# Products of a zeroed tile in f32 with 128 columns in place of bf16 with 512

## The chip, the cores and the metric

The kernel runs on one core of a Trainium2 chip. The core has a matrix engine (TensorE, PE in the profile, with its weight loads as PEld), a vector engine (VectorE, DVE), an activation engine (ScalarE, ACT), a general engine (GpSimd, POOL) and an engine that here only issues transfers (SyncE, SP). Each runs its own list of instructions in order; they wait for each other by semaphores. The metric is the device time of one execution in microseconds. Before the change it is 210.38 us, the median of 3 runs (210.37 to 210.68).

## The reference

Attention over 4 sequences of 768 tokens with 8 heads of 64, followed by two matrix products with a softplus between them:

```python
q, k, v: (4, 8, 768, 64); n_global, n_local = 8, 96
scores = q @ k.T / 8 - slope[h] * dist        # dist = |i - j|, or 96 for a global key outside the window
keep   = (j < 8) | ((i - j >= 0) & (i - j < 96))
a      = softmax(where(keep, scores, -1e9))
x      = (a @ v) as (3072, 512)
h      = x @ w_in                             # w_in: (512, 2048)
g      = max(h, 0) + log1p(exp(-|h|))
out    = g @ w_out                            # w_out: (2048, 512)
```

Inputs and outputs are float32.

## The kernel before, in words

The 3072 tokens are cut into 24 blocks of 128. Two neighbouring blocks form a unit (12 of them), whose q, k and v are loaded as f32, cast to bf16, and q and k are brought into the layout in which the head's dimension lies on the partitions: for the first three units by transposes on TensorE (L792 and L810, products with a permuted identity), for the later ones by transposing transfers. Each block then goes through scores (L897 and L950 `scores`, with a bias that is either added by DVE, L976, or put into PSUM first by a product with the identity, L887 and L931), exp on ACT (L910, L983), the product with v (L1002), the division by the row's sum (DVE, L1013 and L1014) and a transpose back (L1033, evicted at L1038).

Two blocks form a group of 256 tokens (12 groups). `mm1` (L1060) multiplies a group by w_in, eight steps of two 128-column pieces, and ACT makes the softplus of it (exp at L1075, log at L1086). The second product is L1107 for the first two groups, and L522, with sums of blocks made at L452, for the others. w_in and w_out arrive as 16 loads of 512 KB, issued on SP (L640) into a ring of f32 buffers and cast into place (L644).

The order of every engine's work is written out by hand in the string `ORDER`: a name and a letter for the engine each. Semaphores are put in from the reads and writes that each step states. Among the names are `blank`, a memset of a tile by DVE (L1159), and `fill0` to `fill34` (L1234), 35 products of that zeroed tile with itself on TensorE. They stand only in the first 21 us: `fill0` to `fill12` ahead of everything else on TensorE, the other 22 singly, in twos and in threes between the transposes, scores and products with v of the first blocks, the last three (`fill32` to `fill34`) ahead of `a0.2`, the third step of the first group's `mm1`. Each writes the PSUM tile `x_ps`, which nothing reads until a later product has begun it anew. Names that the steps below use: `sb0.0` is the bias product at L887, `trq` and `trk` are transposes, `sc` scores, `pv` the product with v, `xt` the transpose back, `cin` a cast of a w_in piece.

Of the kernel before, what the change touches and what calls it, by code (L numbers as in the profile page):

```python
# [12 lines left out]
F32 = mybir.dt.float32  # L13
BF16 = mybir.dt.bfloat16
# [6 lines left out]
class Program:  # L21
# [6 lines left out]
    def op(self, name, eng, dur, rank, fn, reads=(), writes=(), after=(), dma=None, sync=(), count=1,  # L28
           port=False, alts=None, mutex=None):
        o = Op()  # L30
        o.name, o.eng, o.fn, o.sync, o.ins = name, eng, fn, list(sync), None
        if alts:
            o.eng = self.placed[name]
            assert o.eng in alts, (name, o.eng)
            o.fn = lambda: fn(o.eng)
        assert o.eng == self.placed[name], name
        deps = set(after) | set(sync)
        for t in reads:
            if t in self.writer:
                deps.add(self.writer[t])  # L40
        for t in writes:
            if t in self.writer:
                deps.add(self.writer[t])
            deps.update(self.readers.get(t, ()))
        for t in reads:
            self.readers.setdefault(t, []).append(o)
        for t in writes:
            self.writer[t] = o
            self.readers[t] = []
        deps.discard(o)  # L50
        o.deps = deps
        assert name not in self.ops, name
        self.ops[name] = o
        return o
# [194 lines left out]
def kernel(  # L249
# [11 lines left out]
    nc = tc.nc  # L261
    P = nc.NUM_PARTITIONS
# [29 lines left out]
    const = ctx.enter_context(tc.tile_pool(name="const", bufs=1))  # L292
# [6 lines left out]
    x_ps = ps.tile([P, 512], F32, name="x_ps")  # L299
# [28 lines left out]
    ident = const.tile([P, P], BF16, name="ident")  # L328
    ident_p = const.tile([P, P], BF16, name="ident_p")
    ident_q = const.tile([P, P], BF16, name="ident_q")  # L330
    blank = const.tile([P, 512], BF16, name="blank")
    rel, far, dist = (
        raw_t[NRAW - 1][:, 256 * x : 256 * x + 256].rearrange("p (a t) -> p a t", a=2) for x in range(3)
    )
# [56 lines left out]
    def users(key):  # L391
        return ([pl.writer[key]] if key in pl.writer else []) + list(pl.readers.get(key, ()))
# [838 lines left out]

    def fillers(js):
        def fn():
            nc.tensor.matmul(x_ps[:], blank[:, 0:P], blank[:])  # L1234

        for j in js:
            last = op(f"fill{j}", "PE", 0.216, 1e6 + j, fn, reads=["blank"], after=users(("x",)))
            pl.writer[("x",)], pl.readers[("x",)] = last, []
# [150 lines left out]
```

## Time and profile before

| | |
|---|---|
| median of 3 runs | 210.38 us (210.37 to 210.68) |
| the profiled execution's own time | 210.5 us |
| its span, first to last instruction | 208.6 us |
| PE busy | 201.1 us, 96% |
| ACT, DVE, POOL busy | 172.9, 159.9, 103.9 us |
| the 32 recorded products of the zeroed tile | 11.0 us on PE, 1.2 to 20.6 us |
| weight loads | 2211 |

Lengths are in us where nothing else is said. Products overlap in the pipeline: the length of one (mean 454 ns for the zeroed tile) is longer than the distance from one start to the next, and the distance is what a row of them costs. A bracket behind a row of the timeline says how long the engine sat idle ahead of it and what ended that. The chain of waits is followed back from the last instruction to what released each step.

### The profile page before, as it was taken

How to read it: one execution, taken by the hardware profiler on the slowest of the kernel's cores; microseconds unless marked ns; L12 is line 12 of the kernel's file. 1: busy time of each engine (PE TensorE's matmuls, PEld its weight loads, DVE VectorE, ACT ScalarE, POOL GpSimd, SP SyncE). 2: the span in 40 equal slices, each digit the busy share in tenths (PEclk: the TensorE clock that was granted, in tenths of full speed). 3: DMA queues.
4: the chain of work that ended last, by engine and by line, in shares of the span. 5: the costliest groups of instructions: out<-in, count | busy, mean ns of one | idle time of the engine just before them, and what ended most of it. 6: DMA issues, size and time to landing. Idle time of an engine off the chain costs nothing.

```text
span 208.6 us, 5495 instructions
## 1 busy us (share of the span) xinstructions
PE 201.1 (96%) x2202; PEld 164.7 (79%) x2211; DVE 159.9 (77%) x302; ACT 172.9 (83%) x254; POOL 103.9 (50%) x107
## 2 busy tenths in 40 slices
PE   7999899999998999999999999999999999999993
PEld 2465787666767889888988888888888889888882
DVE  5878889999869896786997897927897784434373
ACT  4788999899998999999799999679879895897300
POOL 4064683327886532546062179865707506623540
PEclk9999999999999999999999999999999999999999
DMA  5999999999999998999899969965641304200205
GB/s 172 365 361 388 387 357 363 336 240 237 205 178 231 240 199 204 244 310 200 198 176 287 245 149 227 249 135 126 103 76 28 126 5 134 71 0 0 104 16 187
DMA packets 70649, 40.99 MB, mean 196 GB/s; under 512 B 30432, under 2 KB 62688, under 8 KB 70624
## 3 DMA queue, kind: packets, MB, share of 16 engines
q1 hardware_dynamic: 69936, 39.99, 79.5%
q10 hardware_dynamic: 688, 0.66, 1.0%
q8 instruction: 17, 0.28, 0.6%
q14 instruction: 8, 0.07, 0.1%
HBM read 27.26 MB, written 6.29 MB: 161 GB/s over the span
## 4 chain that ended last, share of the span: by engine, by line
PE 74%; DMA 11%; DVE 8%; SPq 2%; issue 1%; POOL 1%; ACT 1%; ACTq 0%; POOLq 0%; DVEq 0%
PE h_ps L1060 34%; PE o_ps L522 23%; DMA raw<-in_moe_w_in_dram 5%; PE x_ps L1002 4%; PE s_ps L950 4%; PE s_ps L1107 3%; DMA kT<-kb 3%; DMA raw<-in_v_dram 2%; PE o_ps L1107 2%; PE x_ps L522 2%; DVE z L976 2%; DMA out_dram<-osb 1%; PE s_ps L522 1%; DVE vb L707 1%; SPq L640 1%
## 5 line engine op out<-in xcount | busy, mean ns | idle before, releaser
L1060 PE MATMUL h_ps<-XT,w_in_bf 128*128 128x256 bf16 x768 | 94.0, 273 | 1.3 <-DMA XT<-xs 0.6
L1060 PEld LDWEIGHTS <-w_in_bf 128*128 128x128 bf16 x768 | 73.4, 98 | 12.8 <-DMA XT<-xs 0.7
L1075 ACT ACTIVATE e<-h_ps 128x512 f32<-128x512 f32 x96 | 59.4, 635 | 13.7 <-PE h_ps L1060 13.0
L1086 ACT ACTIVATE g<-e 128x1024 bf16<-128x1024 f32 x48 | 49.6, 1051 | 0.5
L976 DVE TENSOR_TENSOR z<-s_ps,biasA 128x1024 f32<-128x1024 f32 x38 | 45.8, 1217 | 2.6 <-PE s_ps L950 1.9
L983 ACT ACTIVATE pb<-z 128x1024 bf16<-128x1024 f32 (+1 forms) x44 | 43.2, 992 | 1.9 <-DVE z L976 1.4
L452 POOL TENSOR_TENSOR g<-g 128x1024 bf16<-128x1024 bf16 x11 | 24.1, 2194 | 31.1 <-DVE raw L452 30.9
L522 PEld LDWEIGHTS <-g 128*128 128x128 bf16 x320 | 30.8, 98 | 3.6
L452 POOL TENSOR_TENSOR raw<-g 128x1024 bf16<-128x1024 bf16 x8 | 17.5, 2182 | 19.3 <-ACT g L1086 13.3
L522 PEld LDWEIGHTS <-raw 128*128 128x128 bf16 x240 | 22.7, 98 | 2.7
L522 PE MATMUL o_ps<-raw,raw 128*128 128x256 bf16 x192 | 24.4, 273 | 0.0
L452 DVE TENSOR_TENSOR raw<-g 128x1024 bf16<-128x1024 bf16 x22 | 16.8, 770 | 5.6 <-ACT g L1086 3.5
L1002 PEld LDWEIGHTS <-pb 128*128 128x128 bf16 x352 | 16.4, 98 | 4.2 <-ACT pb L983 0.5
L522 PE MATMUL o_ps<-raw,g 128*128 128x256 bf16 x160 | 19.6, 273 | 0.0
L1014 DVE TENSOR_TENSOR xs<-x_ps,rcp 128x256 bf16<-128x256 f32 x40 | 17.0, 424 | 1.4
L1002 PE MATMUL x_ps<-vb,pb 128*128 128x65 bf16 x304 | 15.8, 193 | 0.2 <-DVE xs L1014 0.2
L522 PE MATMUL o_ps<-w_out_bf,g 128*128 128x256 bf16 x128 | 15.8, 273 | 0.0
L675 POOL CAST qb<-raw 128x1024 bf16<-128x1024 f32 x8 | 9.7, 1215 | 10.4 <-DMA raw<-in_q_dram 8.7
L707 POOL CAST vb<-raw 64x512 bf16<-64x512 f32 x20 | 13.6, 680 | 2.3 <-DMA raw<-in_v_dram 1.5
L868 POOL COPY vb<-vb 4x512 bf16<-4x512 bf16 x18 | 11.7, 649 | 5.0 <-PE x_ps L1002 4.3
L1013 DVE RECIPROCAL rcp<-x_ps 128x4 f32<-128x4 f32 x40 | 7.1, 178 | 7.6 <-PE x_ps L1002 7.1
L1234 PE MATMUL x_ps<-blank 128*128 128x512 bf16 x32 | 11.0, 454 | 1.5 <-DVE blank L1159 1.2
(125 smaller groups left out, 225.6 us busy)
## 6 DMA issues: line engine op xcount, KB each, us to landing
raw<-in_v_dram SPq DMA_DIRECT2D x12, 512.0 KB, 5.5
out_dram<-osb SPq DMA_DIRECT2D x22, 256.0 KB, 3.4
raw<-in_q_dram SPq DMA_DIRECT2D x9, 512.0 KB, 5.1
raw<-in_k_dram SPq DMA_DIRECT2D x9, 512.0 KB, 5.9
raw<-in_moe_w_in_dram SPq DMA_DIRECT2D x8, 512.0 KB, 9.1
raw<-in_moe_w_out_dram SPq DMA_DIRECT2D x8, 512.0 KB, 9.2
raw<-in_k_dram SPq DMA_DIRECT2D x6, 256.0 KB, 5.9
raw<-in_q_dram SPq DMA_DIRECT2D x4, 256.0 KB, 7.1
```

What stands on the lines that cost most here:

```text
L452: (nc.vector if eng == "DVE" else nc.gpsimd).tensor_tensor(dst, a[0], b[0], ALU.subtract)
L522: nc.tensor.matmul(psum(j), lhs[:, f // 2, f % 2, :], w(f), start=(f == 0 and not (chain and j in "267")), stop=(f == 7), skip_group_check ...
L707: copy_on[eng](dst, src)
L868: copy_on[eng](vb_of(prev)[sl, :, 0:D], vb_of(first)[sl, :, 0:D])
L976: nc.vector.tensor_tensor(z, src, bias, ALU.add)
L983: nc.scalar.activation(pb[:, 0:nr, :].rearrange("p (y a) b -> p y (a b)", y=2), src, AF.Exp, scale=1.0 / root_d)
L1002: nc.tensor.matmul(xv[:, h, :], pb[:, 4 * (h % 2) + 2 * part + h // 2 if lone else u_all * (2 * (h % 2) + h // 2) + u, :], vb_of(prev if u ...
L1014: nc.vector.tensor_tensor(xs[:, 4 * part : 4 * part + 4, :], xv[:, :, 0:D], rcp[:][:, :, None].to_broadcast([P, 4, D]), ALU.mult,)
L1060: last = nc.tensor.matmul(hv[:, j, :], w_in_bf[:, m, fb * P : fb * P + P], XT[g % NXG][:, m, :], start=(m == 0), stop=(m == NM - 1),)
L1075: nc.scalar.activation(e[:, p % 2, :, :].rearrange("p j (b t r) -> p (j b) r t", b=2, r=2), hb[:].rearrange("p (a r t) -> p a r t", a=4, r=2),
L1086: nc.scalar.activation(gt[:, 2 * p - 2 : 2 * p + 2, :].rearrange("p a t -> p (a t)"), e[:].rearrange("p a j t -> p (a j t)"), AF.Ln, bias=1.0,
L1234: nc.tensor.matmul(x_ps[:], blank[:, 0:P], blank[:])
```

## The change

The zeroed tile becomes 128 x 128 in f32 (512 bytes in a partition) where it was 128 x 512 in bf16 (1024 bytes). Each product takes the whole tile as both operands and writes 128 columns of `x_ps`, where it took 128 columns as weights and all 512 as the moving operand.

```diff
-    blank = const.tile([P, 512], BF16, name="blank")
+    blank = const.tile([P, P], F32, name="blank")
 ...
     def fillers(js):
         def fn():
-            nc.tensor.matmul(x_ps[:], blank[:, 0:P], blank[:])
+            nc.tensor.matmul(x_ps[:, 0:P], blank[:], blank[:])
 
         for j in js:
             last = op(f"fill{j}", "PE", 0.216, 1e6 + j, fn, reads=["blank"], after=users(("x",)))
```

`ORDER` and all other steps stay as they are. In the program's list for TensorE a product of bf16 is two rows, a weight load and the product; a product of f32 is one row, with no load written for it. The first place is the head of TensorE's list (before with -, after with +; the counts and waits stand at the row):

```order
-L1234 LDWEIGHTS blank [waits DVE_49]
-L1234 MATMUL x_ps<-blank 128x512
+L1234 MATMUL x_ps<-blank 128x128 [waits DVE_49]
+L1234 MATMUL x_ps<-blank 128x128 x12
 L887 LDWEIGHTS ident [waits DVE_49,Pool_49]
 L887 MATMUL h_ps_64<-bias_127,ident 128x256 [waits Activation_49]
```

The wait for the memset moves from the load to the product; 13 pairs, of which the first is shown, become 13 rows, still ahead of the bias product of `sb0.0`.

The second place is `fill13`, between `sb0.0` and the first transposes of q, which wait for DVE's cast:

```order
 L887 MATMUL h_ps_65<-bias_127,ident 128x256 [waits Activation_49]
-L1234 LDWEIGHTS blank
-L1234 MATMUL x_ps<-blank 128x512
+L1234 MATMUL x_ps<-blank 128x128
 L792 LDWEIGHTS qb_81 [waits DVE_49]
 L792 MATMUL s_ps_61<-ident_q,qb_81 128x2x32x2 [waits Activation_49]
```

No row around it moves and no wait is added; the same holds at every other place. On DVE one row changes, the memset (counted in 32-bit words there):

```order
 L1384 UNCONDITIONAL_BRANCH
-L1159 MEMSET blank 128x256
+L1159 MEMSET blank 128x128
 L1192 SCALAR_TENSOR_TENSOR raw_80<-raw_80 128x128
 L1195 TENSOR_SCALAR raw_80<-raw_80 128x128
```

It keeps its place and writes half the words. The lists of ACT, POOL and SP are the same.

## The prediction

> **What bounds the kernel now.** I read the page's sums first, then the chain that ended last, then the first 26 us engine by engine, since all 35 of the changed products stand there. The sums and the chain (share of the span by engine):
>
> ```profile
> span 208.6 us, 5495 instructions
> PE 201.1 (96%) x2202; PEld 164.7 (79%) x2211; DVE 159.9 (77%) x302; ACT 172.9 (83%) x254; POOL 103.9 (50%) x107
> PE 74%; DMA 11%; DVE 8%; SPq 2%; issue 1%; POOL 1%; ACT 1%; ACTq 0%; POOLq 0%; DVEq 0%
> ```
>
> TensorE (PE) sets the end. Busy time in stretches (columns: stretch and its length, then busy us and instructions of PE, weight loads, DVE, ACT, POOL, then granted clock, DMA share, GB/s) shows where it could still absorb a delay:
>
> ```profile
> 10.00:20.00 10.00, 9.62 (x128) 6.55 (x130) 8.21 (x21) 8.05 (x14) 5.90 (x8) 1.00 1.08 372
> 20.00:30.00 10.00, 9.24 (x122) 7.47 (x121) 8.69 (x16) 9.58 (x15) 7.01 (x9) 1.00 1.06 381
> 40.00:50.00 10.00, 9.94 (x91) 6.56 (x92) 9.73 (x19) 9.96 (x15) 2.95 (x3) 1.00 1.08 264
> 80.00:100.00 20.00, 20.00 (x238) 17.48 (x236) 14.50 (x30) 18.81 (x27) 8.98 (x7) 1.00 1.20 249
> ```
>
> From 80 us on PE has no gap, so a PE that is late by more than its early waits ends late by about the rest. Up to 30 us the transfers are full (372 and 381 GB/s), and the chain in order of time goes there through the loads, not through the changed products:
>
> ```profile
> 9.70 10.11 DMA raw<-in_moe_w_in_dram
> 19.83 0.69 DVE w_in_bf L644
> ...
> 24.61 1.05 POOL w_in_bf L644
> 25.70 1.92 PE h_ps L1060 x16
> ```
>
> Now the changed products themselves: the group, and its stretches (busy us and count of L1234 alone).
>
> ```profile
> L1234 PE MATMUL x_ps<-blank 128*128 128x512 bf16 x32 | 11.0, 454 | 1.5 <-DVE blank L1159 1.2 <-issue 0.2
> 1.10:5.30 4.20, 4.11 (x10) 1.49 (x11) 1.00 0.75 221
> ```
>
> Three of the 35 have no record. Ten start in the first 4.2 us, one every 0.42 us, though the column of the granted clock says 1.00; afterwards they are quicker, as PE's timeline shows (start, length, count; in brackets the idle time before and who ended it):
>
> ```profile
> 1.19 4.97 PE L1234 MATMUL x_ps<-blank 128*128 128x512 bf16 x13 [1.19 <-DVE blank L1159]
> 5.99 0.60 PE L887 MATMUL h_ps<-bias,ident 128*128 128x256 bf16 x4
> 6.43 0.38 PE L1234 MATMUL x_ps<-blank 128*128 128x512 bf16 x1
> 6.80 0.40 PE L792 MATMUL s_ps<-ident_q,qb 128*128 128x128 bf16 x4
> 7.04 0.38 PE L1234 MATMUL x_ps<-blank 128*128 128x512 bf16 x1
> 8.55 0.40 PE L897 MATMUL h_ps<-qT,kTa 64*128 64x128 bf16 x8 [0.25 <-DVE kTa L795]
> 11.58 0.59 PE L1234 MATMUL x_ps<-blank 128*128 128x512 bf16 x2
> 12.01 0.61 PE L810 MATMUL s_ps<-ident_p,kb 128*128 128x128 bf16 x8
> 17.23 0.59 PE L1234 MATMUL x_ps<-blank 128*128 128x512 bf16 x2
> 17.66 1.91 PE L1060 MATMUL h_ps<-XT,w_in_bf 128*128 128x256 bf16 x16
> 20.59 1.05 PE L1060 MATMUL h_ps<-XT,w_in_bf 128*128 128x256 bf16 x8 [0.24 <-DVE w_in_bf L644]
> 25.03 0.40 PE L1002 MATMUL o_ps<-vb,pb 128*128 128x65 bf16 x8 [0.17 <-DVE xs L1014]
> 25.70 1.92 PE L1060 MATMUL h_ps<-XT,w_in_bf 128*128 128x256 bf16 x16 [0.27 <-POOL w_in_bf L644]
> ```
>
> Two products from 11.58 to 12.01 make 0.215 us each: that is the old price of one at full speed, and 0.42 us before about 5.3 us. The reader is to see that most work behind a group of them follows without a gap: there the products set when it starts.
>
> **The change part by part.** *The zeroed tile.* The memset writes half as many words. Its row, and that of the smallest memset here:
>
> ```profile
> 0.86 0.27 DVE L1159 MEMSET blank<- 128x256 uint32 x1 [0.86 <-PEq L1370]
> L1227 DVE MEMSET raw<- x2: 165/165/165, 3.8 to 4.0; 4x128 f32 x2
> ```
>
> The new one writes 128 words in a partition, as those of 165 ns do, so I take 165 ns against 270: the first product starts 0.11 us sooner (bounds: 0 and 0.27). DVE gains nothing, since its next step waits for POOL's iota:
>
> ```profile
> 1.62 0.29 DVE L1192 SCALAR_TENSOR_TENSOR raw<-raw 128x128 f32<-128x128 f32 x1 [0.49 <-POOL raw L1150]
> ```
>
> *The products, 35 times.* In the program's order a weight load and a product of 512 columns become one row. On the engine it is not one: the compiled instruction list of TensorE holds 2246 loads and 2246 products after the change, where the profile of before counts 2211 loads. Each f32 product is compiled to two pairs of load and product over the same 128 columns. So 35 loads and 35 products are added, and the trace of before has no f32 product to price them by. Bounds from the nearest rows:
>
> - Below: a pair with 128 columns in bf16. Four such take from 6.80 to 7.04, 0.06 us each, although one load is recorded at 98 ns; loads run beside products there.
>
> ```profile
> L792 PEld LDWEIGHTS <-qb x8: 95/98/99, 6.8 to 8.0; 128*128 128x128 bf16 x8
> L792 PE MATMUL s_ps<-ident_q,qb x4: 219/219/230, 6.8 to 7.0; 128*128 128x128 bf16 x4
> ```
>
> Two such pairs are 0.12 us, 0.10 less than now.
>
> - Above: the old price with two loads of 98 ns that nothing hides, 0.215 + 0.196 = 0.41 us, 0.196 more than now.
>
> - Taken: 0.215. Per partition a bf16 product with 512 columns streams 512 x 2 = 1024 bytes; two f32 products with 128 columns stream 2 x 128 x 4 = 1024. By the work that it streams, the pair of pairs is nearest to the old product's row, and each load then has 0.107 us of product to hide behind, more than its 98 ns. At the early half speed both double alike, 0.42 us.
>
> The Trainium skill (FP8 and Floating Point Precision, "TensorE Precision Notes") says that a true FP32 product takes four passes through the array. Four passes at the 0.06 us of the L792 row would be 0.24 us, 25 ns more than now; 22 products behind 6 us would add 0.55 us, which the waits below would take up. The skill has a rule that speaks against this change: by TensorE: Matmul & The Clock Gate, section on weight-path perf modes, the fast weight load is not used for FP32. By that page's plain load, columns / 1.2 per ns, one load would be an estimated 107 ns, as long as the product that should hide it; the sum would stay if it overlaps and go to the upper bound if not. No run here shows either yet.
>
> *What it does to the path.* First 13 products: they start 0.11 us sooner and take as long, so the bias products (now 5.99) come 0.1 us sooner. That is not passed on: the next real step, the transposes at 6.80, waits for DVE's cast of q:
>
> ```profile
> 6.33 0.42 DVE L659 CAST qb<-raw 128x512 bf16<-128x512 f32 x1
> ```
>
> It ends at 6.75, while the product at 6.43 leaves PE free at 6.43 + 0.215 = 6.65: a wait of 0.15 us. The four products between 6.43 and 7.91 and the eighteen behind 11 us keep their length, and so DVE, ACT and POOL, which at 11 to 13 us wait for PE, get their inputs when they do now:
>
> ```profile
> DVE rcp L1013 <- PE o_ps L1002: 1.0, 2, 0.6
> ACT kTa L817 <- DVE kTa L817: 0.6, 1, 0.6
> ```
>
> If the products were longer, these would be late, and behind DVE's late steps stand SP's load issues (SP waited 1.8 us for DVE's xs):
>
> ```profile
> SPq L640 <- DVE xs L1014: 1.8, 1, 1.8
> ```
>
> *Cover.* PE's waits that a delay can use up are 0.15 (6.80) + 0.25 (8.55) + 0.24 (20.59) + 0.27 (25.70) = 0.91 us. The 0.17 at 25.03 I leave out: DVE's xs there would be late too. If this cover is gone, each further microsecond costs a microsecond, for from 80 us on PE has no gap.
>
> *Sum.* -0.11 at the start, used up by the wait at 6.80; 35 times 0.00 to 0.02, at most 0.44 for the 22 behind 6 us, inside 0.91. Nothing is left: the profiled execution, 210.5 us (span 208.6 and 1.9 around it), stays, and the median of the runs shown, 210.38, becomes **210.4**.
>
> **The rivals.**
>
> *A. As summed.* Half of the cover would still take products of 0.235 us; 210.0 to 210.8.
>
> *B. Loads that show (slower).* The f32 load cannot run beside the product ahead of it. For it: the operand is twice as wide, two loads stand where one stood, and no row shows an f32 load. Against it: every bf16 load here hides, even behind products of 0.06 us. Place: first the row of 13, then all groups to 20 us. With both loads open, one product costs 0.42 + 0.196 = 0.62 us until 5.3 us and 0.41 after: 6.7 products from 1.1 to 5.3 us, the other 6.3 in 2.6 us, so the bias products start at 7.9, 1.9 us late. The 22 others add 22 x 0.196 = 4.3. 6.2 - 0.91 = +5.3: 215.7. With one of the two loads open: 8.0 in the first 4.2 us at 0.52, five at 0.313, 0.9 late; 22 x 0.098 = 2.2; 3.1 - 0.91 = +2.2: 212.6. It decides from 0.91 / 35 = 26 ns more for each.
>
> *C. Cheap products.* Both halves run as bf16 pairs, 0.12 us at full speed. Then the 13 end by 1.1 + 13 x 0.24 = 4.2 us, PE stands until the identity is there, the groups at 11 to 17 us end sooner, but the first product with a late weight block still waits for its cast at 20.59 and 25.70, and those for loads that already come at 372 to 381 GB/s. Gain: at most the 0.27 us between these waits, if earlier casts let SP issue sooner; 210.1 to 210.4. Against it: it would make f32 as quick by column as twice bf16, although it streams twice the bytes.
>
> *D. The speed rises later (slower).* Before, a product's pace changed after 4.1 us of them, from 0.42 to 0.215. If f32 products count for less there and PE stays slow to 8.55 us: the last three of the 13 cost 3 x 0.21 more, four other products 0.85, and the real ones up to 8.55 (four with 256 columns, twelve with 128: some 4 x 0.11 + 12 x 0.06 = 1.15) as much again: 2.6 - 0.4 (the waits at 6.80 and 8.55) = +2.2, and 2.2 - 0.51 at 20.59 and 25.70 = +1.7: 212.1. Against it: the array streams as long as before, back to back.
>
> *The change doesn't do what it says* holds for the count: two pairs, not one instruction. A pair is taken every 0.06 us at L792, twice that is under 0.215, so the extra two instructions cost nothing unless B holds.
>
> **How the numbers follow.** A 0.52, B 0.27, C 0.12, D 0.09. What a measurement of this kernel can tell from no change is 0.2%, 0.42 us. A gives no change in 0.46 and a little faster in 0.06; C 0.06 and 0.06; B and D are slower. So faster 0.12, same 0.52, slower 0.36. The range goes from 209.9, under C's and A's ends, to 212.7, over B with one open load and D; left out are B with both loads open (0.12) and a larger gain than any case has (0.05). A's own range is 210.0 to 210.8.
>
> **What would show it.** In the profile after: a group L1234 with f32 and 128x128, twice 35 products if all are recorded, and 2246 loads. A is right if two new products in a row (at 11.58 now) last 0.41 to 0.47 us to the next real product, and the waits at 20.59 and 25.70 for w_in_bf are still there. B shows as gaps between the products that weight loads fill, bias products behind 6.5 us, no wait at 20.59, and everything behind 26 us moved by one amount. C shows as PE idle between 4.3 and 5 us. D shows as products behind 6 us that start as far apart as those before 5 us. Wrong altogether would be this forecast if the end moves while the first product behind 25.70 does not.

## The result, and the profile after

The changed kernel takes 212.53 us (median of 4 runs, 211.84 to 213.31) against 210.38 (with a fourth run of before, 209.98 to 210.68): 1.0104 of before, 95% interval 1.0055 to 1.0154. Timed again beside the last experiments it was 1.0106 (1.0064 to 1.0147). No change was forecast (210.4), and the kernel is slower by about 1%. The traces kept of e2, e9 and e12 below are of executions that ran slow (214.89, 214.63 and 726.11 us), such executions are left out of all ratios, and nothing is read from these three traces.

The page after, in the same parts as before: the span and the engines' busy time; the group of the changed products; the queue that fetches instructions, which reads word for word the same before and after.

```profile
span 210.0 us, 5574 instructions
...
PE 202.2 (96%) x2246; PEld 171.2 (82%) x2246; DVE 160.8 (77%) x302; ACT 173.1 (82%) x254; POOL 103.8 (49%) x107
...
q8 instruction: 17, 0.28, 0.6%
...
PE 62%; DMA 13%; DVE 10%; ACT 8%; issue 2%; SPq 2%; POOL 0%; ACTq 0%; DVEq 0%; POOLq 0%
...
L1234 PE MATMUL x_ps<-blank 128*128 128x128 f32 x70 | 12.4, 320 | 1.1 <-DVE blank L1159 1.1
```

35 products have become 70 records, and 35 loads are added (2211 before): 2246 of each. The chain is less PE (62% where it was 74%) and more DMA, DVE and ACT: the path to the end runs more often through others. The memset's own line after (shortest, median, longest in ns):

```profile
L1159 DVE MEMSET blank<- x1: 165/165/165, 0.8 to 0.8; 128x128 f32 x1
```

PE's timeline after:

```profile
1.05 4.78 PE L1234 MATMUL x_ps<-blank 128*128 128x128 f32 x26 [1.05 <-DVE blank L1159]
5.66 0.60 PE L887 MATMUL h_ps<-bias,ident 128*128 128x256 bf16 x4
6.10 0.39 PE L1234 MATMUL x_ps<-blank 128*128 128x128 f32 x2
6.61 0.40 PE L792 MATMUL s_ps<-ident_q,qb 128*128 128x128 bf16 x4
6.84 0.44 PE L1234 MATMUL x_ps<-blank 128*128 128x128 f32 x2
...
11.65 0.69 PE L1234 MATMUL x_ps<-blank 128*128 128x128 f32 x4
12.17 0.61 PE L810 MATMUL s_ps<-ident_p,kb 128*128 128x128 bf16 x8
...
18.22 1.91 PE L1060 MATMUL h_ps<-XT,w_in_bf 128*128 128x256 bf16 x16
...
20.86 1.03 PE L1060 MATMUL h_ps<-XT,w_in_bf 128*128 128x256 bf16 x8
...
25.76 1.92 PE L1060 MATMUL h_ps<-XT,w_in_bf 128*128 128x256 bf16 x16 [0.27 <-POOL w_in_bf L644]
```

The whole first part went nearly as forecast. The 26 records of the first 13 products end earlier than before (the bias products stand at 5.66, not 5.99), because the first starts sooner and the change of pace comes sooner, near 4.5 us where it was 5.2. Behind 6 us two products cost 12.17 - 11.65 = 0.52 us where they cost 0.43. PE falls back to 0.56 us late at 18.22 (17.66 before), loses the wait at 20.59, and at 25.70 it is 0.06 us late. Up to here that is all that the products themselves cost in this trace.

The loss comes later. From 26 to 48 us both traces run side by side; then PE waits for a transpose of k, at the place where before it had no wait. PE's timeline before:

```profile
49.05 0.62 PE L950 MATMUL s_ps<-qT,kT 64*128 64x128 bf16 x16
```

And after:

```profile
50.02 0.62 PE L950 MATMUL s_ps<-qT,kT 64*128 64x128 bf16 x16 [0.85 <-DMA kT<-kb]
```

The list of DMA issues, asked for the stretch from 44 to 45 us, gives the time from issue to landing of that transpose as its last number, before:

```profile
kT<-kb SPq DMA_TRANSPOSE x1, 4.4
```

And after:

```profile
kT<-kb SPq DMA_TRANSPOSE x1, 5.8
```

It was issued at 44.13 before and at 44.17 after, so it did not start late: it took 1.4 us longer. A wait of 0.64 us at 64.5 in the trace of before takes up most of it (PE is 0.33 us late at 70.8), and the same happens again, to a load of v. The list of DMA issues from 69 to 69.5 us, before:

```profile
raw<-in_v_dram SPq DMA_DIRECT2D x1, 512.0 KB, 5.3
```

And after:

```profile
raw<-in_v_dram SPq DMA_DIRECT2D x1, 512.0 KB, 6.5
```

It is issued 0.30 us late and takes 1.1 us longer, and ACT, behind it, casts it 1.30 us later than before, with exp, log and PE's next product behind that. ACT's timeline before:

```profile
74.63 0.62 ACT L707 CAST vb<-raw 64x512 bf16<-64x512 f32 x1
```

And after:

```profile
75.93 0.62 ACT L707 CAST vb<-raw 64x512 bf16<-64x512 f32 x1 [1.15 <-DMA raw<-in_v_dram]
```

The chain of waits after now runs through that load, with its 6.47 us from issue to landing:

```profile
69.39 6.47 DMA raw<-in_v_dram
```

PE is 1.3 us late at 81.6 and stays so: the span is 210.0 where it was 208.6.

What is different about these transfers? The list of DMA queues, asked for a stretch of two microseconds, shows one packet of 16 KB of instructions in each (columns: packets, MB, share of 16 engines' time). After, from 47 to 49 us (from 71 to 73 us the row is the same with 3.0%):

```profile
q8 instruction: 1, 0.02, 3.7%
```

Before, neither stretch has one; the nearest stand from 51 to 53 and from 74 to 76 us:

```profile
q8 instruction: 1, 0.02, 3.8%
```

3.7% of 16 engines over 2 us is 1.2 us of one engine. There are 17 such packets in either trace. From the first to the last of them, TensorE starts 248 recorded loads and products for each packet, before as after, while DVE, ACT and POOL have 302, 254 and 107 instructions in all: this queue brings TensorE its instructions, a block of them at a time. The first seven packets start, by the trace:

```
before   16.17  26.24  38.63  52.05  61.76  74.34  84.85 ...
after    14.63  24.58  34.65  47.56  59.98  71.55  82.28 ...
```

The change adds 70 instructions to TensorE's list ahead of 21 us. PE therefore comes to each block's border 70 instructions sooner, and the seven fetches shown come 1.5 to 4.5 us sooner, against transfers that are issued nearly where they were. How a fetch makes a transfer late is inferred, since no view names the DMA engine of a packet: if a transfer is spread over the engines and has landed when the last of them is done, the one that a fetch holds for 1.2 us is the last. The packets of the trace fit this. Those of 4 and 256 bytes, most of what moves while the k transpose is under way, stop at 47.8 us, but for two of 4 bytes at 48.73 and 48.74, as the fetch ends (47.56 + 1.19 = 48.75); the landing is recorded at 49.98. The Trainium skill (Runtime: NRT & Kernel Launch, "Instruction fetch mechanics") describes such fetches, in blocks of 16 KB or 256 instructions through a DMA queue of the engine's own, and calls their cost "mostly hidden". The period agrees with the traces (248 recorded loads and products, with some instructions of TensorE not among them). That the cost is hidden holds for PE here, in whose list of waits no fetch stands, but not for the transfers beside it.

### The profile page after: what moved, and what is told of

The parts are those of the page before. It is cut to its first block, busy times and chain, and to the rows that moved or that the text cites. A ratio compares the mean times of both kernels' runs of the same rounds, so it can differ in the third digit from the quotient of the medians.

```text
span 210.0 us, 5574 instructions
## 1 busy us (share of the span) xinstructions
PE 202.2 (96%) x2246; PEld 171.2 (82%) x2246; DVE 160.8 (77%) x302; ACT 173.1 (82%) x254; POOL 103.8 (49%) x107
## 4 chain that ended last, share of the span: by engine, by line
PE 62%; DMA 13%; DVE 10%; ACT 8%; issue 2%; SPq 2%; POOL 0%; ACTq 0%; DVEq 0%; POOLq 0%
PE h_ps L1060 29%; PE o_ps L522 21%; DMA raw<-in_moe_w_in_dram 5%; DVE z L976 4%; PE s_ps L950 3%; PE x_ps L1002 3%; ACT pb L983 3%; DMA raw<-in_v_dram 3%; DMA raw<-in_q_dram 3%; DMA kT<-kb 3%; ACT e L1075 2%; PE x_ps L522 2%; PE s_ps L1107 2%; ACT g L1086 2%; PE s_ps L522 1%
## 5 line engine op out<-in xcount | busy, mean ns | idle before, releaser
L1234 PE MATMUL x_ps<-blank 128*128 128x128 f32 x70 | 12.4, 320 | 1.1 <-DVE blank L1159 1.1
L675 POOL CAST qb<-raw 128x1024 bf16<-128x1024 f32 x8 | 9.2, 1150 | 8.5 <-DMA raw<-in_q_dram 7.8
```

The source lines that it names most:

```text
L1234: nc.tensor.matmul(x_ps[:, 0:P], blank[:], blank[:])
```

## The experiments

The theory from the two traces (F in the expectations) is that the moved fetches make the kernel slower. Its rival (L) is the price of the f32 products themselves: the first pair of a group costs 0.05 to 0.10 us more, and PE is 0.56 us late at the product that stood at 17.7 us. In all experiments only the zeroed tile's products are changed; nothing reads them. What is varied is how many instructions they are and, in e4 and e8, how many of the late ones are f32 or there at all. The code cuts show the lines that differ; the kernels are changed nowhere else but in how the loop hands over the number j.

| kernel | f32 | instructions more | of before | 95% interval |
|---|---|---|---|---|
| the change | all 35 | 70 | 1.0104 | 1.0055 to 1.0154 |
| e1 bf16 in halves | none | 70 | 1.0079 | 1.0052 to 1.0106 |
| e2 first 13 in quarters | none | 78 | 1.0075 | 1.0051 to 1.0100 |
| e3 plus one fetch | none | 256 | 1.0003 | 0.9974 to 1.0032 |
| e4 f32, plus one fetch | 22 late ones | 256 | 1.0034 | 1.0010 to 1.0058 |
| e5 one fetch and 70 | none | 326 | 1.0106 | 1.0073 to 1.0138 |
| e6 half a fetch | none | 128 | 1.0086 | 1.0052 to 1.0119 |
| e7 three quarters | none | 192 | 1.0027 | 1.0004 to 1.0051 |
| e8 none late | none, 22 left out | 0 | 1.0015 | 0.9993 to 1.0038 |
| e9 the change again | all 35 | 70 | 1.0106 | 1.0064 to 1.0147 |
| e10 bf16 twin of e4 | none | 256 | 1.0014 | 0.9991 to 1.0037 |
| e11 seven eighths | none | 226 | 1.0037 | 1.0008 to 1.0065 |
| e12 first 13 in halves | none | 26 | 1.0033 | 1.0003 to 1.0062 |

### e1: the same count of instructions without f32

```diff
-            nc.tensor.matmul(x_ps[:], blank[:, 0:P], blank[:])
+            n, c = (2, 256)
+            for _ in range(n):
+                nc.tensor.matmul(x_ps[:, 0:c], blank[:, 0:P], blank[:, 0:c])
```

> All 35 products stay bf16 and on 512 columns, but each is issued as two pairs of load and product of 256 columns: 70 more instructions for TensorE than before, as many as the change adds, no f32, the memset as before. Theory F (fetches): the change is slower because 70 more instructions move TensorE's 16 KB instruction fetches to other moments (14.63 instead of 16.17 us, 47.56 instead of 52.05), where one falls into the k transpose that the scores at 50 us wait for; so here 211.8 to 213.3 us, fetches near 14.5 and 47.5 us, and a wait of PE for kT near 50 us. Theory L (length): the change is slower because an f32 product's first load behind bf16 work shows (some 0.05 us for each group, PE 0.55 us late at 17.7 us); here nothing of that, so 210.0 to 210.7 us.

Measured: 212.28 us, 1.0079 of before. There is no f32 in it, the memset is the old one, and PE reaches the product behind the wait at 25.7 us at 25.79. The k transpose lands late all the same, and PE waits at the same place (5.8 us in the list of issues, as in the change). PE's timeline in e1:

```profile
50.05 0.62 PE L950 MATMUL s_ps<-qT,kT 64*128 64x128 bf16 x16 [0.85 <-DMA kT<-kb]
```

Its fetches start at 14.46, 24.45, 34.81 and 47.82 us. The rival L cannot make this: the loss is there without f32. Here too the first loss is mostly taken up (PE is 1.0 us late at 50.0, 0.1 at 64.6) and comes again (0.8 at 81.2). This second time the load of v is issued 0.66 us late and takes 5.6 us, and ACT waits 0.3 us for it, so its second loss does not come about quite as in the change.

### e2: only the first 13 are touched

The loop is that of e1, with other numbers:

```diff
+            n, c = (4, 128) if j < 13 else (1, 512)
```

> Only the first 13 products are cut, each into four pairs with 128 columns (78 more instructions, all ahead of 6 us); the 22 others are as before. F: fetches where the change has them, a few instructions earlier still, so slower by about 1% (211.5 to 213.5 us) though nothing behind 6 us is touched. L: no f32 and no longer products, 210.0 to 210.7 us.

Measured: 212.11 us, 1.0075. Instructions that all stand ahead of the first bias product cost 1.7 us, which no work of theirs explains.

### e3 and e5: one whole fetch more, and 70 beyond it

```diff
+            n, c = (11 if j < 11 else 10, 40) if j < 13 else (1, 512)
```

This is e3, with 141 pairs for the first 13 products; e5 has 176 pairs with 32 columns there.

> The first 13 products become 141 pairs with 40 columns: 256 instructions more than before, one whole 16 KB fetch; the 22 others are as before. The zeroed tile's product is smaller in work, but nothing reads it. F: from 6 us on the fetches come at the same places of the program as before the change, so 210.0 to 210.7 us, with fetches near 16.2, 26.2, 38.6 and 52 us and one more ahead of 6 us. If instead more instructions as such cost time, this is the slowest of all, above 212.5 us. L: 210.0 to 210.7 us too.

> The first 13 products become 176 bf16 pairs with 32 columns: 326 instructions more than before, that is one whole fetch of 256 and the 70 of the change; the 22 later ones are as before. F: the fetches stand behind 10 us where the change has them, so slow again, 211.5 to 213 us, with a fetch near 47.5 us and a wait of PE for kT near 50 us. If the time followed the count of instructions, it would be above the 210.57 us of 256 more only by what 70 of them cost in the row of warm-up products, some tenths; if only the late f32 products mattered, 210.0 to 210.7 us.

Measured: e3 210.57 us, 1.0003; e5 212.49 us, 1.0106. With 256 instructions more the time is that of before, with 70 beyond these it is slow again. Counted instructions cannot do that; a period of 256 can. In e3 the k transpose is back at its old length and the wait is gone, in e5 both are as in the change. What happens ahead of 26 us does not decide it: PE reaches the product that stood at 25.70 at 25.73 in e3, 25.76 in the change, 25.79 in e1 and 25.95 in e5. PE's timeline in e3, where the list of issues gives 4.4 us again:

```profile
49.07 0.62 PE L950 MATMUL s_ps<-qT,kT 64*128 64x128 bf16 x16
```

The list of PE's waits in e5 (us in total, times, longest):

```profile
PE s_ps L950 <- DMA kT<-kb: 0.8, 1, 0.8
```

e3 also shows the fetch at work by itself. It has one that before had not, from 7 to 9 us (at 7.68), when the loads are queued one behind the other. POOL's first cast of k waits for loads, here in POOL's timeline of e3 (which names a load of v as the one that came last):

```profile
12.00 0.61 POOL L675 CAST kb<-raw 128x512 bf16<-128x512 f32 x1 [6.97 <-DMA raw<-in_v_dram]
```

And before:

```profile
10.82 0.82 POOL L675 CAST kb<-raw 128x512 bf16<-128x512 f32 x1 [5.82 <-DMA raw<-in_k_dram]
```

It starts 1.18 us later. By the trace, the loads of q and k that landed at 9.38, 10.05 and 10.77 land at 10.53, 11.22 and 11.94, all 1.15 to 1.17 us later. They are level again (18.42 against 18.46) where before has its own fetch, at 16.17. All of this is taken up by the waits ahead of 26 us.

### e4 and e10: the f32 products with the fetches put back

The cut is against the kernel after the change:

```diff
-    blank = const.tile([P, P], F32, name="blank")
+    blank = const.tile([P, 256], F32, name="blank")
+    blank_bf = blank.bitcast(BF16)
 ...
+            if j >= 13:
+                nc.tensor.matmul(x_ps[:, 0:P], blank[:, 0:P], blank[:, 0:P])
+                return
+            for _ in range(9 if j < 11 else 10):
+                nc.tensor.matmul(x_ps[:, 0:48], blank_bf[:, 0:P], blank_bf[:, 0:48])
```

e10 has bf16 at every place: 119 pairs with 48 columns, and then two pairs with 256.

> The 22 later products are f32 with 128 columns as in the change (44 more instructions), and the first 13 become 119 bf16 pairs with 48 columns (212 more): 256 in all, one whole fetch. The tile has 256 words in a partition as before. F: back to 210.0 to 210.8 us in spite of the f32 products, since the fetches come at the old places. L: the f32 groups keep their price, PE 0.4 to 0.6 us late at 17.7 us, and the time stays at 211.8 to 213.3 us.

> The first 13 products as 119 bf16 pairs with 48 columns, and the 22 later ones bf16 as two pairs with 256 columns: the same 256 instructions more, at the same places, as the kernel with f32 late products that took 1.0034 of before, but without f32. F alone says that that one's 0.3% is from where the fetches stand between 6 and 21 us: 1.003 here too. If the f32 products' first loads cost it: 1.000.

Measured: e4 211.12 us, 1.0034; e10 210.51 us, 1.0014. Two thirds of the loss are gone with the 22 late f32 products still in. Between F (at most 210.8) and L (at least 211.8), e4 lies in neither range, nearer to F. Whether f32 itself costs the rest cannot be told: e10 came out between its two forecasts (1.000 and 1.003), and the intervals of e4 and e10 overlap from 1.0010 to 1.0037. Timing the change again (e9) was to tell it too, 1.008 by F alone and 1.010 to 1.012 with a price of f32 on top; 1.0106 lies in the second, and its interval reaches down over the first. So f32 has a price of its own between none and some 0.5%.

### e6, e7, e11, e12: other counts

The first 13 products are cut into 77, 109, 126 and 26 pairs with 86, 60, 48 and 256 columns.

> The first 13 products become 77 bf16 pairs with 86 columns: 128 instructions more, half a fetch; the others as before. F: fetches half a period earlier than before the change (near 11.5, 21.5, 32, 44.5 us); the time depends on what they meet there, between 209.5 and 213 us; every load in flight at a fetch before 40 us lands some 1.2 us late until the place where before the change had its own fetch. A count theory expects half of what 256 cost, so 210.5 us.

> The first 13 products become 109 bf16 pairs with 60 columns: 192 instructions more, three quarters of a fetch; the others as before. F: fetches near 9.5, 19, 29, 41.5 and 54 us; between 209.5 and 213 us, and not between the times of 128 and 256 more by any rule of counting. A count theory expects 210.5 to 210.6 us.

> The first 13 products as 126 bf16 pairs with 48 columns: 226 instructions more, which puts the fetches 30 instructions later than before the change; the others as before. F: fetches near 8.5, 17.7, 27.5, 40 and 53 us, none in the first k transposes of 44 to 48.5 us, so 209.6 to 210.9 us.

> The first 13 products as two bf16 pairs with 256 columns: 26 instructions more; the others as before. F: fetches some 26 instructions earlier than before (near 15.5, 25.3, 37 and 50.5 us): the one near 50.5 is behind the k transpose that lands at 48.5, so 210.0 to 211.2 us, less than the 212.1 to 212.5 of 70 to 78 more. A count theory expects at most 210.5.

Measured: 1.0086, 1.0027, 1.0037 and 1.0033. None is faster than before. The time does not follow the count: 128 cost three times what 192 cost. In e6 PE waits only 0.2 us for k's transposes, and another transfer is hit: the fetch at 120.36 us falls into a transpose of the attention's output, which takes 4.0 us where it took 2.5 and for which PE waits at 123.5 us, where before it had no wait. PE's waits in e6:

```profile
PE h_ps L1060 <- ACT e L1075: 1.3, 2, 1.1
...
PE h_ps L1060 <- DMA XT<-xs: 0.6, 1, 0.6
...
PE s_ps L950 <- DMA kT<-kb: 0.2, 1, 0.2
```

The longest one, 1.1 us for ACT's exp at 71.2, leaves PE 0.35 us late; behind the wait at 123.5 it is 0.8 us late to the end.

e11 and e12 are misses in size: medians of 211.34 and 211.45 us where at most 210.9 and 211.2 were expected, because only the first k transposes were looked at there. In e11 that part held (no wait of PE for kT), and what else costs it 0.4% was not found; e12 has no trace that can be read. Nor is one trace the whole of a kernel: the trace of e7 is of an execution of 212.36 us where the median is 210.88, and single executions of before, with its fetches where they are, run from 209.81 to 212.30 us beside the last experiments. The medians show what a count costs, a trace where one execution lost its time.

### e8: the late products left out

```diff
+            n, c = (3 if j < 9 else 2, 190) if j < 13 else (0, 0)
+            for _ in range(n):
+                nc.tensor.matmul(x_ps[:, 0:c], blank[:, 0:P], blank[:, 0:c])
```

> The 22 later warm-up products are left out, and the first 13 become 35 bf16 pairs with 190 columns, so that TensorE has as many instructions as before; nothing reads what is left out. F: the fetches of before behind 21 us, 44 instructions earlier between 6 and 21 us; 209.8 to 210.8 us if PE keeps its full speed, since its waits at 20.6 and 25.7 us end with casts of loaded weights. If the later products are needed to keep the speed, PE's products between 8 and 20 us are twice as far apart and the time is above 211 us.

Measured: 210.87 us, 1.0015 (0.9993 to 1.0038). So neither outcome was clean. Without the late products PE stands still for 1.0 us ahead of the second piece of w_in, and then it is slow. Its timeline in e8:

```profile
18.07 2.78 PE L1060 MATMUL h_ps<-XT,w_in_bf 128*128 128x256 bf16 x14 [1.01 <-DVE w_in_bf L644]
```

Busy time in stretches of e8, where the column behind the five engines is the granted clock:

```profile
19.00:20.00 1.00, 1.00 (x6) 0.70 (x5) 0.66 (x3) 0.76 (x1) 0.81 (x1) 0.50 1.05 385
```

The clock is 0.50, where it is 1.00 before in the same stretch. Fourteen products take 2.78 us where sixteen took 1.91 before. PE is 1.0 us late at 21.6 and 0.5 us late at 28; most of it goes into later waits. By these two traces the late products keep the speed, but the kernel hardly needs it there.

## Why the prediction was right or wrong

**What bounds the kernel** held as far as it went: the end follows PE, and a delay of PE beyond its waits is passed on (1.3 us at 81.6, 1.4 at the end). It left out that transposes and loads land just in time behind 40 us, with no spare for one that is 1.4 us longer.

**The memset** was right to the nanosecond: 165 ns, first product 0.14 us sooner (0.11 forecast). The bias products came 0.33 us sooner, not 0.1: the change of pace, which rival D feared later, came some 0.7 us sooner, which these runs do not tie to f32 (in e1 it comes near 5.5 us). The wait for q's cast took it up as forecast.

**The price of a product** was right in a row and a little low behind other work. Two pairs in a row take 0.11 us each at full speed and 0.21 at the early one, 0.22 and 0.43 for a product: the 0.215 and 0.42 that were taken from the streamed bytes. By the four passes that the Trainium skill states (FP8 and Floating Point Precision, "TensorE Precision Notes"), 0.24 was worked out; 0.22 agrees, since four times the 0.055 us of a bf16 pair is just that. The Trainium skill's rule on the fast weight load (TensorE: Matmul & The Clock Gate, section on weight-path perf modes) shows as well: an f32 load is recorded at 192 ns where a bf16 one lasts 98. The sum let each load hide with 98 ns, and the 107 ns estimated from that page is not the recorded length either; yet in a row a load starts every 0.11 us and is hidden, since the records overlap. It shows in the first pair of a group. Behind products with 128 columns or fewer that pair takes 0.165 to 0.213 us (the group at 6.84 lasts 0.44), behind the bias products with 256 columns 0.11 (the one at 6.10 lasts 0.39). That part of rival B was real and small: 0.05 to 0.10 us for ten of the eleven groups from 6 us to the product that stood at 17.66, which comes 0.56 us late.

**The cover** was right: 0.56 us late at 18.22 became 0.06 at 25.76.

**The step that failed** is the last of the sum, the added instructions at no price. "35 loads and 35 products are added", and then "the extra two instructions cost nothing unless B holds": they were priced by the time in which PE takes them and by nothing else. That they are also fetched, by DMA beside the kernel's data, stood on the page of before as the row of the instruction queue, 17 packets and 0.28 MB, and was not read. Its share of 0.6% looks like nothing; a single packet is 1.2 us of one engine of 16. With no f32 at all, the 70 instructions alone cost 0.8% (e1), and 256 nothing that could be measured (e3).

**The rivals.** The measured 212.53 lies inside the range given, 209.9 to 212.7, and that is luck: the range reached so far only for B and D, and neither made the time. B gave 212.6 for one open load, which is the measured time by another mechanism: its marks (bias products behind 6.5 us, everything behind 26 us moved by one amount) are absent. C and D did not occur: no idle PE at 4.3 us, and products behind 6 us in full pace. The mark for a forecast that is wrong altogether, the end moves while the first product behind 25.70 does not, is what was seen.

## What to carry to other kernels

Count the instructions that an edit adds or removes on each engine, in the compiled list, even where they cost the engine no time: they can move the fetches of that engine's list against every transfer behind them (shown here for TensorE's list alone). On a kernel whose transfers land just in time, compare an edit only with a variant that has the same count modulo 256 (here 70 more cost 0.8%, 256 more nothing that could be measured), or the phase of the fetches is taken for the effect of the edit. Where a transfer takes longer though it was issued on time, look for the instruction queue in the same stretch.

## What the runs showed that was not expected

One packet of 16 KB of instructions takes 0.9 to 2.1 us (half of them 1.0 to 1.2), and a transfer that runs through it took 1.1 to 1.5 us longer in the cases read (w_in's second load landed at 17.16 instead of 15.93, k's transpose at 49.98 instead of 48.54), though at the first of these the fetch is only 16 of some 450 KB that move in 1.2 us at 372 GB/s. A zeroed f32 product with 128 columns is compiled to four instructions instead of two and costs what a bf16 one with 512 costs, 0.22 us, and 0.05 to 0.10 us more if bf16 products with 128 columns or fewer stand ahead of it.
